# A scan layer followed by a gated feed-forward layer on one core: decay rows copied in the layout they are read in, and scan work moved between VectorE and GpSimd

## The chip, the cores and the metric

The kernel runs on one core of one Trainium2 chip. The core has TensorE (PE, with its weight loads shown apart as PEld), VectorE (DVE), ScalarE (ACT), GpSimd (POOL) and SyncE (SP, which here only issues transfers). The metric is the device time of one execution in microseconds, the median of several runs.

## What is computed

The first layer is a chunked scan of the Mamba-2 kind over 4 batches x 8 heads, sequences of 768 positions, head size 32 and state size 16. The second layer multiplies each of the 3072 rows of 256 by w_in, gates the result with its cosine, and multiplies it by w_out.

```python
batch, n_heads, seq, head_dim, d_state = (4, 8, 768, 32, 16)
for c in range(nc):
    cum = np.cumsum(la, axis=-1)                       # la = log(clip(a)) in the chunk
    M = einsum('bhin,bhjn->bhij', Cc, Bc) * exp(cum_i - cum_j) * causal
    y_intra = einsum('bhij,bhjd->bhid', M, xc)
    y_inter = einsum('bhin,bhnd->bhid', Cc, state) * exp(cum)[..., None]
    y[:, :, sl] = y_intra + y_inter
    Bx = einsum('bhjn,bhjd->bhjnd', Bc, xc) * exp(cum_last - cum_j)
    state = exp(sum(la)) * state + sum(Bx, axis=2)
x = y.transpose(0, 2, 1, 3).reshape(3072, 256)
h = x @ w_in                                           # 256 x 2048
out = (h * np.cos(h)) @ w_out                          # 2048 x 256
```

All of it is in 32-bit floating point.

## The kernel before

The sequence is cut into 6 chunks of 128 positions, each of two units of 64 (W). One chunk of the scan gives yT, the transposed input of the feed-forward layer for 4 x 128 rows. The feed-forward layer of chunk c runs in 16 steps, n = 16c + f with f from 0 to 15, and while it runs, the scan of chunk c+1 is threaded between its operations. One loop over n (L1114) records the instructions of all engines; each engine then works through its own list in that order, and waits only for data and for buffers.

One step n of the feed-forward layer:

- first(n) (L662): TensorE multiplies a block of w_in with one unit of yT into hp(n), one PSUM bank. Two banks take turns, so hp(n+2) needs hp(n) to have been read for the last time. In the runs of steps listed in `runs` (L1034) first7 (L757) does it instead, with 7 products of 128x128 in place of 8, a fast matrix multiplication. It reads differences of weights (wid, from differ_in, L734 on, made by GpSimd) and differences of y (yd, from differ_y, L745). A step belongs to unit f // 8 of the chunk, so the runs f = 9 to 13 of chunks 2 to 4 read the differences of the second unit only; the last run (steps 81 to 93) reads both.
- wind_k (ScalarE, L679), wind_w (VectorE, L685) and gate (ScalarE, L694) bring hp into range and take the cosine; gated (VectorE, L699) multiplies it with hp into gT(n). From chunk 1 on differ(n) (GpSimd, L724, L726, L727) forms the differences gd(n).
- second(n) runs two steps later. For chunk 0 it is a plain product with w_out (L808), after that seven (L848), whose products are read in the order 1, 2, 6, 7, 5, 4, 3 (1, 2, 7, 5, 6, 4, 3 in a run); products 1 and 2 need gT, 7, 5 and 6 need the first two operations of gd. After the last step of a unit ScalarE copies the sums out of PSUM into ps (L860, L861), and `rest` (L868) adds them up in four operations (L873), which the loop hands to GpSimd one per step where it can (L1197 on), or all four to VectorE.

The scan of a chunk from chunk 2 on:

- a is clipped into la and cut (L951 on), stored to memory (a_all, a_cut) and read back broadcast over partitions. load_arow reads the decays of one unit, from which decays0 scans lam (VectorE, L387). load_along reads whole chunks; `reaches` (L579) scans exp(cum) out of them, two scans of 64 per sequence (L586).
- turn_blocks transposes B and C (VectorE, L594), turn2 cuts C for the two heads of a strip (ScalarE, L603) and makes rT, the product of C with the reach (VectorE, L605). inner2 forms the inner products, weights (VectorE, L477) multiplies them with lam.
- add_state (VectorE, L510) adds the decayed state of the unit before, in four operations. open2 and finish2 sum y in PSUM, which ScalarE copies to yT.

Chunks 0 and 1 come from unit-wise functions. reach_unit (L439) scans the reach of one of the units 2 and 3 at a time, at step 9 and step 17, from alongs that load_unit_along filled.

`steps` (L1006) is a table written by hand: for each chunk the step f at which each piece is recorded. Work on VectorE in a step stands in the list `behind`: one piece before gated, the others after it.

Of the kernel before, what the change touches and what calls it, by code (L numbers as in the profile page):

```python
# [25 lines left out]
def kernel(  # L26
# [51 lines left out]
    ones = const.tile([P, P], FP32, name="ones")  # L78
    V.memset(ones, 1.0)
# [10 lines left out]
    a_all = dram.tile([NB, H, S], FP32, name="a_all")  # L90
    a_cut = dram.tile([NB, H, S], FP32, name="a_cut")
# [68 lines left out]
    def load_arow(k):  # L160

        arows[k] = t = rows.tile([P, H, P], FP32, tag="arow", name="arow").rearrange(
            "p h i -> p (h i)").rearrange("p (q h i) -> p q h i", q=2, h=H)
        i = k % 2
        if i:
            G.memset(t[:, :, :, 0:1], 0.0)
        for s in range(2):
            nc.sync.dma_start(
                out=t[s * W:(s + 1) * W, :, :, i:].rearrange("p q h i -> p (q h) i"),
                in_=a_cut[2 * s:2 * s + 2, :, k * W + i:(k + 1) * W].rearrange("q h i -> (q h) i")  # L170
                .unsqueeze(0).to_broadcast([W, 2 * H, W - i]))

    def load_unit_along(k):

        for p in range(2):
            for s in range(2):
                nc.sync.dma_start(
                    out=alongs[k][:, 2 * p + s, 1:],
                    in_=a_all[2 * s + p, :, k * W:(k + 1) * W].unsqueeze(1).to_broadcast([H, N, W]))

    def load_along(c, seqs=range(NB)):

        if c >= NC:
            return
        if c not in along:
            along[c] = rows.tile([P, NB, P], FP32, tag="along", bufs=2, name="along")
        for b in seqs:
            s = b // 2
            for qs, rs in turns_of[s]:
                hs = slice(2 * qs.start, 2 * qs.stop)  # L190
                nc.sync.dma_start(
                    out=along[c][rs, b], in_=a_all[b, hs, c * P:(c + 1) * P].unsqueeze(1)
                    .to_broadcast([hs.stop - hs.start, N, P]))
# [7 lines left out]
    lead, along1, reach1 = (ms[2][:, i * NB * (W + 1):(i + 1) * NB * (W + 1)]  # L201
                            .rearrange("p (b i) -> p b i", b=NB) for i in range(3))
    reachs = {1: reach1, 2: along1, 3: reach1}
    alongs = {k: ms[3][:, (k - 2) * NB * (W + 1):(k - 1) * NB * (W + 1)]
              .rearrange("p (b i) -> p b i", b=NB) for k in (2, 3)}
# [89 lines left out]
    for s in range(2):  # L295
        load_x(1, s)
    fetch("out", 0)
    nc.sync.dma_start(
        out=a_in, in_=a.rearrange("(u b) h (c p) -> (b h c) u p", u=NU, p=P))
# [80 lines left out]
    def decays0(k, p, i=0, n=1):  # L380

        if p == i == 0:
            lams[k] = scan.tile([P, 2, H, W], FP32, tag="lam", bufs=4, name="lam")
        flat = "p h i -> p (h i)"
        hs = slice(i * H // n, (i + 1) * H // n)
        rows_ = spread.pop((k, p, i)) if k < 2 else arows[k][:, p]
        V.tensor_tensor_scan(out=lams[k][:, p, hs].rearrange(flat), data0=rows_.rearrange(flat),  # L387
                             data1=unit0[:, hs].rearrange(flat), initial=0.0,
                             op0=ALU.mult, op1=ALU.add)
# [49 lines left out]
    def reach_unit(k):  # L439

        flat = "p b i -> p (b i)"
        V.tensor_tensor_scan(
            out=reachs[k].rearrange(flat), data0=alongs[k].rearrange(flat),
            data1=lead.rearrange(flat), initial=0.0, op0=ALU.mult, op1=ALU.add)

    def turn_unit(k):

        tp = pair("tp")[:, 0].rearrange("p (k q i) -> p k q i", k=2, q=2)
        for i, of in enumerate((bs, cs)):
            for p in range(2):  # L450
                PE.transpose(tp[:, i, p], of[k][:, p], ident)  # L451
        bTs[k] = scan.tile([P, 2, 2, P], FP32, tag="turned", bufs=2, name="turned0")[:, 0]
        ACT.copy(out=bTs[k], in_=tp[:, 0])
        cuts[k] = scan.tile([P, 2, 2, P], FP32, tag="cT2", bufs=2, name="cT2")
        for t in range(2):
            ACT.activation(cuts[k][:, t], tp[:, 1], AF.Copy, scale=slot[:, t:t + 1])
        rTs[k] = t = scan.tile([P, NB, W], FP32, tag="rT", name="rT")
        V.tensor_tensor(out=t, in0=tp[:, 1].rearrange("p q (s i) -> p (q s) i", s=2),
                        in1=reachs[k][:, :, 1:], op=ALU.mult)
# [45 lines left out]
    def add_state(k):  # L505

        for s in range(2):
            for p in range(2):
                i = k % 2 * W + W - 1
                V.scalar_tensor_tensor(out=after[k][:, s, p], in0=after[k - 1][:, s, p],  # L510
                                       scalar=reach[k // 2, s][:, p, i:i + 1],
                                       in1=after[k][:, s, p], op0=ALU.mult, op1=ALU.add)

    def finish0(k):
# [44 lines left out]
        def add():  # L559
            dec = scan.tile([P, 2, 2, 2 * D], FP32, tag="whole", bufs=1, name="whole")  # L560
            r4 = reachs[k].rearrange("p (q s) i -> p s q i", s=2)
            for s in range(2):
                G.tensor_tensor(out=dec[:, s], in0=old[:, s],
                                in1=r4[:, s, :, W:].to_broadcast([P, 2, 2 * D]), op=ALU.mult)
# [14 lines left out]
    def reaches(c, b):  # L579

        s, p = divmod(b, 2)
        if p == 0:
            reach[c, s] = scan.tile([P, 2, P], FP32, tag="reach", name="reach")
        for k in range(2):
            i = slice(k * W, (k + 1) * W)
            V.tensor_tensor_scan(out=reach[c, s][:, p, i], data0=along[c][:, b, i],  # L586
                                 data1=ones[:, 0:W], initial=1.0, op0=ALU.mult, op1=ALU.mult)

    turned, ys = {}, {}
# [8 lines left out]
    def turn2(c, s):  # L598

        tp = turned.pop((c, s))  # L600
# [3 lines left out]
        rT = scan.tile([P, 2, P], FP32, tag="rT", name="rT")  # L604
        V.tensor_tensor(out=rT, in0=tp[:, 1], in1=reach[c, s], op=ALU.mult)  # L605
        part[c, s] = (tp[:, 0], cT, rT)

    def inner2(c):

        g = [pair("g") for _ in range(2)]  # L610
        for k, p, s, q in ((k, p, s, q) for k in range(2) for p in range(2) for s in range(2)
                           for q in range(4)):
            bT, cT, _ = part[c, s]
# [9 lines left out]
    def open2(c):  # L623

        ys[c] = y = [pair("y") for _ in range(2)]
        for k, p, s, q in ((k, p, s, q) for k in range(2) for p in range(2) for s in range(2)
# [3 lines left out]
                      rhs=part[c, s][2][r, p, k * W:(k + 1) * W], start=(k == p == 0), stop=False,  # L630
# [4 lines left out]
    def finish2(c):  # L635

        y = ys.pop(c)
# [107 lines left out]
    def differ_y(c, i, eng, us=slice(0, 2)):  # L745
# [6 lines left out]
        a_ = (y12, y22, y22, y21)[i]  # L752
# [195 lines left out]
    la = const.tile([RB, NU, P], FP32, name="la")  # L948
    cut = const.tile([RB, NU, P], FP32, name="cut")

    def clip_cut():  # L951
        G.tensor_scalar(out=cut, in0=a_in, **clip)
        G.memset(cut[:, :, 0:1], 0.0)
        store_a(a_cut, cut)

    def clip_all():
        G.tensor_scalar(out=la, in0=a_in, **clip)

    def store_a(dst, src):
        nc.sync.dma_start(  # L960
            out=dst.rearrange("(u b) h (c p) -> (b h c) u p", u=NU, p=P), in_=src)
# [16 lines left out]
    def rest_of_loads():  # L978
        store_a(a_all, la)
# [7 lines left out]
        load_unit_along(2)  # L987
# [9 lines left out]
        load_unit_along(3)  # L997
        for s in range(2):
            load_x(3, s)
        for k in (4, 5):  # L1000
            for s in range(2):
# [4 lines left out]
    steps = {c: dict(reach=(5, 6), turn=(6, 7), inner=8, weigh=(9, 10), state=(-NF, 12),  # L1006
                     decays=(8, 11, 13, 14), along=(12, 13)) if c == 2 else
             dict(reach=(1, 2), turn=(3, 4), inner=5, weigh=(6, 7), state=(0, 5),
                  decays=(2, 8, 14, 15), along=(6, 7)) for c in range(2, NC)}
# [24 lines left out]
    runs = [*(range(NF * c + 9, NF * c + 14) for c in range(2, NC - 1)),  # L1034
            range(NC * NF - 15, NC * NF - 2)]
    sevens = {n: r for r in runs for n in r}
    late, at_ = [], {}

    def first_of_seven(n):
# [7 lines left out]
        to_ = at_["hp"] if i % 3 == (n > NF * (NC - 1)) else bank([P, TB], "hp", "h")  # L1047
# [63 lines left out]
    for k in (2, 3):  # L1111
        G.memset(alongs[k][:, :, 0:1], 0.0)
    rest_of_loads()
    for n in range(AHEAD, NC * NF + LAG):  # L1114
        c, f = divmod(n, NF)
        if n < NC * NF:
# [9 lines left out]
            if n in (NF - 1, NF):  # L1126
                load_along(2, (2 * (n == NF), 2 * (n == NF) + 1))
            for e, i in chunks_at(n, "along"):
                load_along(e + 1, (2 * i, 2 * i + 1))
# [9 lines left out]
            take_y = finish2(c + 1) if closing else None  # L1139
            if n not in sevens:  # L1140
# [4 lines left out]
            for e, s in chunks_at(n - 1, "turn"):  # L1145
                turn2(e, s)
            for k in units_at(n, 2):
# [10 lines left out]
            if joins:  # L1158
# [4 lines left out]
            behind += [lambda k=2 * c - 1 + i: add_state(k) for c, i in chunks_at(n, "state")]  # L1163
            behind += [lambda c=c, b=2 * s + p: reaches(c, b) for c, s in chunks_at(n, "reach")
                       for p in range(2)]
# [28 lines left out]
            for i, at in enumerate((4, 5, 6, 6) if 2 <= c < NC - 1 else ()):  # L1194
                if at == f:
                    differ_y(c, i, G, slice(1, 2))
            if unsummed and (c > 1 or summed[0]):  # L1197
# [13 lines left out]
        for start, js in zip((2 * NF - 5, 3 * NF - 3, 4 * NF - 3),  # L1211
                             (slice(1, 6), slice(0, 1), slice(6, NJ))):
# [21 lines left out]
        for k in units_at(n, 1):  # L1234
            reach_unit(k)
# [37 lines left out]
```

## Time and profile before

| | |
|---|---|
| three runs | 364.08, 364.23, 365.22 us |
| profiled execution | 364.44 us, its span 362.7 us, TensorE clock granted 0.998 |
| TensorE busy | 357.0 us (98%), 4070 matmul records |
| VectorE busy | 276.0 us (76%), 504 |
| ScalarE busy | 184.0 us (51%), 352 |
| GpSimd busy | 239.7 us (66%), 387 |
| transfers | 96624 packets, 26.43 MB, of which 86624 under 512 B |

Each 32-bit product counts as two records in the trace. The span is cut in stretches by chunk below: busy us of each engine.

| stretch, us | TensorE | VectorE | ScalarE | GpSimd |
|---|---|---|---|---|
| 0 to 17.7 | 16.05 | 14.00 | 7.60 | 9.70 |
| 17.7 to 81 | 63.14 | 52.96 | 42.64 | 46.30 |
| 81 to 140 | 59.00 | 47.39 | 27.33 | 44.52 |
| 140 to 197 | 57.00 | 42.48 | 27.64 | 38.19 |
| 197 to 254 | 57.00 | 42.51 | 27.60 | 38.10 |
| 254 to 311 | 57.00 | 40.26 | 26.19 | 33.34 |
| 311 to 362.7 | 47.84 | 36.42 | 24.99 | 29.54 |

In a timeline each line has the start, the duration, the engine, the line of the kernel, the operation, the tile written and those read, the shapes and the count of merged instructions; in brackets the idle time before it and what ended that.

### The profile page before, as it was taken

Reading aid. Unit: us, or ns where it says so; the run is one execution under the profiler, and the core shown is the slowest. Engines: PE = TensorE matmul, PEld = TensorE weight load, DVE = VectorE, ACT = ScalarE, POOL = GpSimd, SP = SyncE. Lnnn points to the kernel's source line nnn. Section 1 sums busy time; section 2 is a strip of 40 time slices with the busy share of each in tenths; the row PEclk is TensorE's granted clock in tenths of the full one; section 3 lists DMA queues with packets and bytes.
Section 4 is the critical chain, followed back from the end, with each engine's and each line's share of the span. In section 5 each row is a group of like instructions: output and inputs, shape, how many; then the busy total and the mean of one; then the engine's idle time right before and its main releaser. Section 6 shows DMA issues by size and latency. Waiting matters only on the chain.

```text
span 362.7 us, 10240 instructions
## 1 busy us (share of the span) xinstructions
PE 357.0 (98%) x4070; PEld 326.0 (90%) x4070; DVE 276.0 (76%) x504; ACT 184.0 (51%) x352; POOL 239.7 (66%) x387
## 2 busy tenths in 40 slices
PE   8999999999999999999999999999999999999995
PEld 4788888889999999999989999999999999999995
DVE  7779998488876987878766877875776776688864
ACT  3597656544454346534536533545553544444552
POOL 5567767699666677674786666686666465475572
PEclk9999999999999999999999999999999999999999
DMA  7984997666583429113228202110001001001001
GB/s 138 246 284 141 189 196 122 85 125 98 134 129 58 99 51 135 14 34 76 53 53 119 23 3 75 28 33 11 0 2 31 0 3 33 0 3 29 3 17 44
DMA packets 96624, 26.43 MB, mean 73 GB/s; under 512 B 86624, under 2 KB 92480, under 8 KB 96576
## 3 DMA queue, kind: packets, MB, share of 16 engines
q1 hardware_dynamic: 95328, 25.38, 34.9%
q8 instruction: 32, 0.52, 0.6%
q10 hardware_dynamic: 1248, 0.39, 0.5%
q14 instruction: 16, 0.13, 0.1%
HBM read 22.36 MB, written 3.34 MB: 71 GB/s over the span
## 4 chain that ended last, share of the span: by engine, by line
PE 96%; DMA 2%; DVE 1%; issue 0%; ACT 0%; POOL 0%; DVEq 0%
PE o L848 35%; PE hp L672 33%; PE o L808 8%; PE m L772 7%; PE hp L772 5%; DMA bc<-in_C_dram 2%; PE y L641 2%; PE g L615 1%; PE y L489 1%; PE y L629 1%; PE g L468 1%; PE y L537 1%; PE y L527 1%; PE o L900 0%; PE tp L451 0%
## 5 line engine op out<-in xcount | busy, mean ns | idle before, releaser
L672 PE MATMUL hp<-yT,w_in 128*128 128x256 f32 x544 | 129.6, 382 | 0.1
L672 PEld LDWEIGHTS hp<-yT,w_in 128*128 128x128 f32 x544 | 99.0, 190 | 13.8 <-issue 1.4
L724 POOL TENSOR_TENSOR gd<-gT 128x256 f32<-128x256 f32 x79 | 58.1, 735 | 76.9 <-DVE gT L699 61.8
L694 ACT ACTIVATE w<-w,quarter 128x512 f32<-128x512 f32 x96 | 69.4, 723 | 65.8 <-DVE w L685 65.7
L685 DVE SCALAR_TENSOR_TENSOR w<-hp,k 128x512 f32<-128x512 f32 x96 | 65.8, 686 | 45.4 <-ACT k L679 45.2
L679 ACT ACTIVATE k<-hp 128x512 int32<-128x512 f32 x96 | 57.2, 596 | 68.6 <-PE hp L672 60.3
L699 DVE TENSOR_TENSOR gT<-hp,w 128x512 f32<-128x512 f32 x96 | 65.6, 683 | 12.2 <-ACT w L694 8.3
L848 PE MATMUL o<-words,gd 128*128 128x128 f32 x474 | 66.0, 275 | 0.0
L848 PEld LDWEIGHTS o<-words,gd 128*128 128x128 f32 x474 | 59.4, 192 | 0.0
L848 PE MATMUL o<-w_out,gT 128*128 128x128 f32 x316 | 50.4, 278 | 0.0
L848 PEld LDWEIGHTS o<-w_out,gT 128*128 128x128 f32 x316 | 45.4, 191 | 3.1
L726 POOL TENSOR_TENSOR gd<-gT,gd 128x128 f32<-128x128 f32 x79 | 39.6, 501 | 6.2
L727 POOL TENSOR_TENSOR gd<-gT,gd 128x128 f32<-128x128 f32 x79 | 39.0, 493 | 6.2
L848 PE MATMUL o<-w_out,gd 128*128 128x128 f32 x158 | 30.6, 276 | 0.0
L848 PE MATMUL o<-words,gT 128*128 128x128 f32 x158 | 30.6, 275 | 0.0
L808 PE MATMUL o<-w_out,gT 128*128 128x256 f32 x128 | 30.0, 380 | 0.0
L387 DVE TENSOR_TENSOR_SCAN lam<-arow,unit 128x512 f32<-128x512 f32 x20 | 29.9, 1496 | 0.1
L808 PEld LDWEIGHTS o<-w_out,gT 128*128 128x128 f32 x128 | 24.2, 190 | 3.6 <-POOL w_out L283 0.4
L848 PEld LDWEIGHTS o<-words,gT 128*128 128x128 f32 x158 | 24.0, 192 | 0.0
L848 PEld LDWEIGHTS o<-w_out,gd 128*128 128x128 f32 x158 | 24.0, 192 | 0.0
L772 PE MATMUL m<-m,words 128*128 128x128 f32 x168 | 23.4, 276 | 0.0
L772 PE MATMUL hp<-yT,w_in 128*128 128x128 f32 x112 | 21.7, 275 | 0.0
(130 smaller groups left out, 463.6 us busy)
## 6 DMA issues: line engine op xcount, KB each, us to landing
words<-in_moe_w_in_dram SPq DMA_DIRECT2D x8, 512.0 KB
words<-in_moe_w_out_dram SPq DMA_DIRECT2D x8, 512.0 KB
xr<-in_x_dram SPq DMA_DIRECT2D x24, 128.0 KB
arow<-a_cut SPq DMA_DIRECT2D x10, 256.0 KB
arow<-a_cut SPq DMA_DIRECT2D x10, 252.0 KB
out_dram<-sum SPq DMA_DIRECT2D x18, 128.0 KB
bc<-in_B_dram SPq DMA_DIRECT2D x24, 64.0 KB
blocks<-in_B_dram SPq DMA_DIRECT2D x16, 32.0 KB
```

The source lines that it names most:

```text
L387: V.tensor_tensor_scan(out=lams[k][:, p, hs].rearrange(flat), data0=rows_.rearrange(flat), data1=unit0[:, hs].rearrange(flat), initial=0.0 ...
L672: PE.matmul(to_[:, e], lhsT=w_in[:, k, fs], rhs=y[:, k], start=(k == 0), stop=(k == KT - 1), skip_group_check=True)
L679: ACT.activation(k, hp[n], AF.Copy, bias=0.25, scale=INV_2PI)
L685: V.scalar_tensor_tensor(out=w, in0=hp[n], scalar=INV_2PI, in1=k, op0=ALU.mult, op1=ALU.subtract)
L694: ACT.activation(cos, cos, AF.Sin, bias=quarter, scale=TWO_PI)
L699: V.tensor_tensor(out=gT[n], in0=hp.pop(n), in1=cos, op=ALU.mult)
L724: G.tensor_tensor(out=d[:, 0:2], in0=g[:, 1:2].to_broadcast([P, 2, P]), in1=g[:, 3::-3], op=ALU.subtract)
L726: G.tensor_tensor(out=d[:, 2], in0=g[:, 0], in1=d[:, 0], op=ALU.subtract)
L727: G.tensor_tensor(out=d[:, 3], in0=g[:, 2], in1=d[:, 2], op=ALU.subtract)
L772: PE.matmul(dst[q], lhsT=w[q], rhs=y_[q], start=(q in (6, 1, 7)), stop=True, skip_group_check=True)
L808: PE.matmul(o[c, u][:, t], lhsT=g[:, 2 * e + t], rhs=w_out[:, 2 * j + e], start=(j == e == t == 0), stop=(j == NJ - 1 and e == 1), skip_gr ...
L848: PE.matmul(at[q], lhsT=a_[q], rhs=w[q], start=(j == 0 and q in starts), stop=(j == NJ - 1), skip_group_check=True)
```

## The change

- *Copies of a.* a_all and a_cut get new layouts in memory. A row of a_all holds, for a chunk and a pair of sequences, four units of 64 with one element ahead of each (set to 0 in la), so 260 elements in a row; a row of a_cut holds the decays of all 8 heads of a unit. They are read back in rows of 1040 and 2048 bytes. The memsets of arow and of alongs go; a_in is loaded by four transfers, la is stored by two.
- *Reach.* The scan runs over 260 elements at once, restarted by the tile lead (1 ahead of each unit, 0 elsewhere), for a pair of sequences. A chunk needs two such scans instead of eight of 64. For units 2 and 3 reach_unit(s) does pair s for both units, at steps 9 and 10.
- *State and rT on GpSimd.* From chunk 3 on add_state2 multiplies the old state by its decay and, a step later, adds it: two GpSimd operations of 128x256 for four on VectorE. rT becomes scale2, on GpSimd from chunk 3 on.
- *Differences of y.* In chunks 2 to 4 those of the second unit stay on GpSimd, at f = 1 and 2 instead of 4 to 6. Those of the first unit are added, on VectorE at f = 0, from PSUM.
- *Sums.* The condition under which `rest` goes to GpSimd leaves out f = 2, 3, 4 after chunk 1; where it does not hold, the branch below it gives all four operations to VectorE (outside a run of seven).
- *Order.* From chunk 3 on: reach at f = 5, 6 (1, 2 before), transposes at -1, 1 (3, 4), cuts at 3, 4 (4, 5), rT at 6, 7 (4, 5), state at 2, 7 (0, 5), the first scan of lam at 5 (2). The differences of weights for columns 1 to 5 are made in three pieces instead of one.

```diff
     def load_arow(k):
-        arows[k] = t = rows.tile([P, H, P], FP32, tag="arow", name="arow")...
-        i = k % 2
-        if i:
-            G.memset(t[:, :, :, 0:1], 0.0)
-        for s in range(2):
+        arows[k] = t = rows.tile([P, 2, H * W], FP32, tag="arow", name="arow")
+        for q in range(2):
             nc.sync.dma_start(
...
+                out=t[:, q],
+                in_=a_cut[:, k % 2, q, k // 2].unsqueeze(1).to_broadcast([2, W, H * W]))
...
+    def add_state2(k):
+        dec = scan.tile([P, 2, 2, 2 * D], FP32, tag="whole", bufs=1, name="whole")
+        flat = "p s q d -> p (s q) d"
+        G.tensor_tensor(out=dec.rearrange(flat), in0=after[k - 1].rearrange(flat),
+                        in1=reach[k // 2][:, :, k % 2, W:].to_broadcast([P, NB, 2 * D]),
+                        op=ALU.mult)
+        return lambda: G.tensor_tensor(out=after[k], in0=after[k], in1=dec, op=ALU.add)
...
+    def reaches(c, s):
+        if s == 0:
+            reach[c] = scan.tile([P, NB, 2, W + 1], FP32, tag="reach", bufs=1, name="reach")
+        V.tensor_tensor_scan(
+            out=reach[c][:, 2 * s:2 * s + 2].rearrange("p b k i -> p (b k i)"),
+            data0=along[c][:, s],
+            data1=lead.rearrange("p b i -> p (b i)"), initial=0.0, op0=ALU.mult, op1=ALU.add)
...
+    def scale2(c, s, eng):
+        r2[c, s] = rT = scan.tile([P, 2, P], FP32, tag="rT", name="rT")
+        eng.tensor_tensor(out=rT.rearrange("p q (k i) -> p q k i", k=2),
+                          in0=turned.pop((c, s))[:, 1].rearrange("p q (k i) -> p q k i", k=2),
+                          in1=reach[c][:, 2 * s:2 * s + 2, :, 1:], op=ALU.mult)
...
-             dict(reach=(1, 2), turn=(3, 4), inner=5, weigh=(6, 7), state=(0, 5),
-                  decays=(2, 8, 14, 15), along=(6, 7)) for c in range(2, NC)}
+             dict(reach=(5, 6), turn=(-1, 1), cut=(3, 4), scale=(6, 7), inner=5, weigh=(6, 7),
+                  state=(2, 7), decays=(5, 8, 14, 15), along=(6, 7)) for c in range(2, NC)}
...
+            for i in range(4 if f == 0 and 2 <= c < NC - 1 else 0):
+                differ_y(c, i, V, slice(0, 1), ypsum)
...
-            for i, at in enumerate((4, 5, 6, 6) if 2 <= c < NC - 1 else ()):
+            for i, at in enumerate((1, 1, 2, 2) if 2 <= c < NC - 1 else ()):
                 if at == f:
                     differ_y(c, i, G, slice(1, 2))
-            if unsummed and (c > 1 or summed[0]):
+            for e, s in chunks_at(n, "scale"):
+                if e > 2:
+                    scale2(e, s, G)
+            for add in adds:
+                add()
+            adds[:] = [add_state2(2 * e - 1 + i) for e, i in chunks_at(n, "state") if e > 2]
+            if unsummed and (c > 1 and f not in (2, 3, 4) or summed[0]):
                 unsummed[0](range(summed[0], summed[0] + 1), G)
...
-        for start, js in zip((2 * NF - 5, 3 * NF - 3, 4 * NF - 3),
-                             (slice(1, 6), slice(0, 1), slice(6, NJ))):
+        for start, js in zip((2 * NF - 5, 2 * NF - 1, 2 * NF + 8, 3 * NF - 3, 4 * NF - 3),
+                             (slice(2, 5), slice(1, 2), slice(5, 6), slice(0, 1), slice(6, NJ))):
```

## The prediction

> **What bounds the kernel now.** I read the busy shares and the slices first, then the chain of waits, then the list of waits, and last the timelines of single engines around the places that the diff edits.
>
> ```profile
> PE 357.0 (98%) x4070; PEld 326.0 (90%) x4070; DVE 276.0 (76%) x504; ACT 184.0 (51%) x352; POOL 239.7 (66%) x387
> PE   8999999999999999999999999999999999999995
> PE 96%; DMA 2%; DVE 1%; issue 0%; ACT 0%; POOL 0%; DVEq 0%
> ```
>
> TensorE is busy in all but the first and the last slice, and the chain that ended last is TensorE for 96%. Cut into stretches, the windows show TensorE busy for 16.05 of the first 17.7 us, for 63.14 of the next 63.3, for every one of the 57.00 us of each later chunk, and for 47.84 of the last 51.7. Its clock is granted at 0.998. So from 17.7 us on there is next to nothing to win: the waits of TensorE behind another engine after that point are these.
>
> ```profile
> PEld o L808 <- POOL w_out L283: 0.4, 1, 0.4
> ...
> PEld y L527 <- DVE w L685: 0.3, 1, 0.3
> ...
> PEld hp L672 <- DVE gT L699: 0.3, 1, 0.3
> ```
>
> With two of 0.2 us on the first products of hp they make 1.4 us, all in chunk 0. The diff adds, drops and reorders no TensorE instruction. What it can do is make TensorE wait. So the question at each edit is a margin: how long before TensorE reads a tile does VectorE or GpSimd finish it?
>
> Two margins recur in each step of 3.29 us. VectorE multiplies gT(n) out of the PSUM bank that TensorE needs for hp(n+2), and GpSimd forms gd(n) from gT(n) (L724, L726, L727) for the products o(n), two steps later. The chunk taken for the working is chunk 3; chunks 2 and 4 run the same 57 us earlier and later.
>
> ```profile
> 197.34 0.69 DVE L685 SCALAR_TENSOR_TENSOR w<-hp,k 128x512 f32<-128x512 f32 x1 [1.05 <-ACT k L679]
> ...
> 198.89 0.69 DVE L699 TENSOR_TENSOR gT<-hp,w 128x512 f32<-128x512 f32 x1
> ...
> 205.93 0.68 DVE L699 TENSOR_TENSOR gT<-hp,w 128x512 f32<-128x512 f32 x1
> ```
>
> Step 49 (first three fields: start, duration, engine) shows that from the start of w to the end of gT takes 199.58 - 197.34 = 2.24 us, sine on ScalarE included. gT(51) ends at 206.61, and hp(53) starts at 207.88 in TensorE's timeline: a margin of 1.2 us.
>
> **The change part by part.** The sum is made against the profiled execution, 364.44 us (span 362.7 and 1.7 around it); the median of the runs shown is 0.2 us lower.
>
> *Start.* VectorE loses the memset of ones (0.17 us). It sits ahead of a copy (L324, 1.83 to 2.42) that runs until GpSimd's own copy is done (2.34), and the chain goes through the transfer of C until 6.9 us. So 0 to -0.17; I take 0. The load of a_in becomes four: three more at 0.47 us (its row on SP) push the following fetches by 1.4 us. The first of these, issued at 13.17, is read by ScalarE at 22.55, after other work without a wait; on SP nothing else is queued behind but fetches read later still. 0; bare of that cover, at most 1.4 once.
>
> *Chunk 0.* The one scan that served unit 3 at step 17 (L442) moves to step 10, as two scans of a pair each now serve units 2 and 3. It stands between gT(10) and w(11). The row is 1.15 us in the mean, from 0.67 (L429, fed from PSUM) to 1.39. Before rT of step 11 VectorE idles 0.3 us for ScalarE, and gT(11), at 59.27, is 1.2 us ahead of hp(13). Even 1.39 - 0.3 = 1.1 fits. 0. GpSimd loses memsets of arow (0.12 each) and gains one strided memset of la (0.35, by that of cut), ahead of the w_out piece on which TensorE waits 0.4: -0.1 to +0.2, I take 0.
>
> *Transfers.* arow comes in rows of 2 KB where it came in rows of 256 B, along in 1040 B where it was 512 B. After 6.9 us TensorE waits for no transfer, so 0. The blocks of sequences must land earlier: turn_blocks moves to f = -1 and 1, its last load is issued at 189.5 and read at about 198. Small-packet traffic ahead of it shrinks; 0.
>
> *Step 48 (f = 0).* Between gT(47) and w(48) come two transposes (1.13 the pair) and four differences read from PSUM; the nearest row is L785, 128x128 with one operand in PSUM, 0.29. 1.13 + 4 x 0.29 = 2.3 us against 2.06 us of idle time there. w(48) is 0.2 us later, with 1.6 us of margin, and the state additions (0.95 here) behind it are gone. In chunk 2 the idle time is 1.3, so w(32) is 1.0 later, of which 0.6 is won back since the four state additions between w and gT (1.55) go. 0. Those four results have no reader in chunks 2 to 4: the runs of seven products cover steps f = 9 to 13 only, which read the second half.
>
> *Step 50 (f = 2).* Here the new condition on f sends the four sums of the last output (L873) past GpSimd to VectorE, between gT(50) and w(51); a wait of w(51) holds ScalarE's sine, gT(51) and hp(53). The scan of lam goes from this step, so gT(50) ends at 200.60 (k ready) + 2.27 (step 49: 197.31 to 199.58) = 202.87. The nearest row for the sums is four VectorE operations of 128x256, all in SBUF, right behind a gT and with a gd beside them:
>
> ```profile
> 304.17 0.69 DVE L699 TENSOR_TENSOR gT<-hp,w 128x512 f32<-128x512 f32 x1 [1.33 <-ACT w L694]
> 304.78 1.28 DVE L754 TENSOR_TENSOR m<-yT 128x256 f32<-128x256 f32 x2
> 305.98 1.27 DVE L754 TENSOR_TENSOR m<-yT,m 128x256 f32<-128x256 f32 x2
> 307.17 0.68 DVE L685 SCALAR_TENSOR_TENSOR w<-hp,k 128x512 f32<-128x512 f32 x1
> ```
>
> That is 2.39 us. w(51) starts at 202.79 + 2.39 = 205.18, gT(51) ends at 207.42, hp(53) at 207.88 does not wait: 0, with 0.4 to spare. The low bound is four at 0.42 (rT, L605, alone): also 0. The high bound is the row of the same sums in chunk 1:
>
> ```profile
> 126.97 0.56 DVE L873 TENSOR_TENSOR sum<-ps 128x256 f32<-128x256 f32 x1
> 127.57 2.98 DVE L873 TENSOR_TENSOR sum<-ps,sum 128x256 f32<-128x256 f32 x3
> ```
>
> 3.5 us there, beside a GpSimd difference of 1.73 us. By it gT(51) ends at 208.53, 0.7 us late, three times: +2.1. I take 0, since beside these sums run only gd and short differences, as at 304.
>
> [...]
>
> *Steps 53 to 56 (f = 5 to 8).* The reach scan of the second pair stands before w(55), where VectorE idles 0.45: 1.15 - 0.45 = 0.7 us later, gT(55) 221.3 instead of 220.66. GpSimd's queue up to gd(56) then is
>
> ```profile
> 220.80 0.73 POOL L724 TENSOR_TENSOR gd<-gT 128x256 f32<-128x256 f32 x1 [0.55 <-DVE gT L699]
> 221.61 0.46 POOL L726 TENSOR_TENSOR gd<-gT,gd 128x128 f32<-128x128 f32 x1
> 222.14 0.46 POOL L727 TENSOR_TENSOR gd<-gT,gd 128x128 f32<-128x128 f32 x1
> 223.76 0.64 POOL L393 TENSOR_TENSOR sc<-bc,lam 128x256 f32<-128x256 f32 x1 [1.16 <-DVE lam L387]
> 225.78 0.73 POOL L724 TENSOR_TENSOR gd<-gT 128x256 f32<-128x256 f32 x1 [1.39 <-PE o L848]
> ```
>
> with rT, the decayed state and its addition added, each 0.73 (L566, 128x256). gd(55) from 221.4 for 1.8 us; the scan lam(56) now falls on it and holds one of its operations by 0.8 (an L726 at 125.47 took 1.25 beside a scan, 0.46 alone); then 3 x 0.73 + 0.64: 226.8, where gd(56) started at 225.78. TensorE reads its first part at 227.66: 226.8 + 0.73 = 227.5, just in time. Chunk 2 has one more difference of weights there (128x128, 0.46): 0.4 late. Chunk 4 has no sc: early. Sum +0.4. Bounds: without the collision 0; with two collisions 1.2 + 0.8 + 0.2 = 2.2.
>
> In all 364.44 + 0.4 = 364.84 by the profiled execution, 364.6 by the median.
>
> **The rivals.** (1) No change that can be told from none, as worked out. For it: 1.2 to 1.6 us of margin nearly everywhere, and a TensorE that did not wait before.
> (2) Slower through VectorE: the sums at f = 2 become the bound from 2.8 us on, when w(51) starts after 205.6. At the row of chunk 1, 364.2 + 2.1 + 0.4 = 366.7. For it: the only row of these very instructions. Against: the 1.73 us GpSimd difference beside it there.
> (3) Slower through GpSimd: gd(40), gd(56) and gd(72) late by two collisions each, 364.2 + 2.2 = 366.4. For it: the queue is full to 0.1 us. [...]
> (4) Faster: lighter transfers and GpSimd memsets take away the waits of chunk 0 and nothing else is lost: 364.2 - 1.4 = 362.8 for all of them, 363.5 for half. Against: the scan added at step 10 and the unchanged order of the w_out additions.
>
> **How the numbers follow.** What a measurement of this kernel tells from no change is about 0.3%, 1.1 us: below 363.1 is faster, above 365.3 slower. Chances: (1) 0.54, (2) 0.20, (3) 0.16, (4) 0.10. Of (4) 0.07 lies below 363.1; the rest joins (1) as no change, 0.57, and (2) and (3) make 0.36 for slower. The price is that of (1), 364.6. The range reaches down to half of (4), 363.5, and up to (2), 366.7.
>
> **What would show it.** After: TensorE's instruction count and busy time the same within 0.5 us; no wait of hp on gT at steps 37, 53, 69; sums of about 2.4 us on VectorE at f = 2; gd(40) starting at about 170.4 with o(40) waiting some 0.4 for it. The forecast is wrong if TensorE shows gaps over 0.5 us at f = 4 or 8, or if the time to 17.7 us moves by more than 0.3.

## The result, and the profile after

The changed kernel takes 403.19 us (median of four runs, 399.88 to 404.71), where the kernel before took 364.55 beside it: a ratio of 1.105 (95% interval 1.098 to 1.112), slower by about 39 us. The profiled execution is 403.34 us with a span of 401.5. The forecast was 364.6, and all of its four cases lie below 367.

The page of the changed kernel: its busy times, three rows of its 40 slices (PE, TensorE's busy share in tenths; PEclk, the clock it was granted, in tenths of full speed; DMA, the mean busy share of the 16 DMA engines) and the chain that ended last:

```profile
PE 369.8 (92%) x4070; PEld 334.6 (83%) x4070; DVE 267.5 (67%) x473; ACT 183.5 (46%) x352; POOL 243.4 (61%) x395
...
PE   8999879895579988969999989999999999999996
...
PEclk9999999997869998978999999999999999999999
DMA  7883493711261261224511244200101001000102
...
PE 60%; DMA 13%; SPq 13%; DVE 4%; issue 3%; POOL 3%; ACT 3%; DVEq 0%; ACTq 0%; POOLq 0%
```

The chain was TensorE for 96% and is so for 60%; transfers (DMA) and SP's issuing of transfers (SPq) have taken 13% each. The number of matmul records is the same. The holes in TensorE's row lie in slices 5 to 24 of 10 us each, that is between 40 and 241 us, and through most of them the DMA engines are busy for one to four tenths. So transfers are late while most DMA engines are idle. What the engines wait for, in the list of waits (total, times, longest):

```profile
DVE lam L376 <- DMA arow<-a_cut: 19.2, 5, 7.9
...
PE hp L672 <- DVE gT L699: 16.3, 8, 4.7
...
DVE turned L589 <- DMA blocks<-in_C_dram: 6.8, 2, 3.5
PE g L478 <- DMA xr<-in_x_dram: 6.7, 2, 6.5
...
ACT mag L245 <- DMA words<-in_moe_w_out_dram: 6.5, 2, 6.0
...
ACT mag L245 <- DMA words<-in_moe_w_in_dram: 6.2, 2, 3.3
```

None of these transfers appears in the waits of the kernel before. arow is one that the diff edits; blocks, xr and words are not, nor were their bytes changed. SyncE's timeline around the first two loads of arow:

```profile
33.91 1.17 SPq L163 DMA_DIRECT2D arow<-a_cut  x2
35.20 2.84 SPq L221 DMA_DIRECT2D words<-in_moe_w_in_dram  x1
38.09 7.22 SPq L107 DMA_DIRECT2D bc<-in_B_dram  x2
```

The two loads are issued in 1.17 us (1.30 in the kernel before). The two issues of bc behind them take 7.22, against 2.35 in the kernel before: SP is held up. What the DMA engines do meanwhile is seen in the view of the transfers, cut to 36 to 38 us (packets; then queue, packets, MB, share of 16 engines):

```profile
DMA packets 50, 0.10 MB, mean 51 GB/s; under 512 B 0, under 2 KB 0, under 8 KB 50
...
q1 hardware_dynamic: 50, 0.10, 13.1%
```

13.1% of 16 engines is 2.1 engines. Those were busy for 0.131 x 16 x 2 us = 4.2 us with 50 packets of 2 KB: 0.084 us each. The two loads of a unit are 256 such packets, by estimate 256 x 0.084 / 2 = 10.7 us on two engines. In the diff, the source of one load was [64 copies, 16 rows, 64] and is now [2, 64 copies, 512]: its slowest dimension counts 2, as many as the engines that are busy. That gave the author's theory for the experiments, not shown up to here: the loads of arow run on 2 of the 16 engines because of that 2, and other transfers that need these two, and SP's queue behind them, come late. Loads that keep only so few engines busy are called confined below.

A transfer that the diff leaves alone is late in landing as well, not in its issue only:

```profile
49.22 0.66 ACT L245 ACTIVATE mag<-words 128x512 f32<-128x512 f32 x1 [3.28 <-DMA words<-in_moe_w_in_dram]
```

This is the twelfth piece of weights that ScalarE reads, and the twelfth that is fetched is the one whose issue ended at 38.04 above. It landed some 11.2 us after that; in the kernel before the same piece is read at 44.89 without a wait.

The path from a late load to the end, in the timelines of VectorE and TensorE:

```profile
93.71 1.22 DVE L376 TENSOR_TENSOR_SCAN lam<-arow,unit 128x512 f32<-128x512 f32 x1 [7.87 <-DMA arow<-a_cut]
94.85 0.67 DVE L699 TENSOR_TENSOR gT<-hp,w 128x512 f32<-128x512 f32 x1
```

```profile
85.99 1.89 PE L672 MATMUL hp<-yT,w_in 128*128 128x256 f32 x8
...
95.57 3.78 PE L672 MATMUL hp<-yT,w_in 128*128 128x256 f32 x8 [4.73 <-DVE gT L699]
```

The scan of lam stands ahead of gT on VectorE and waits 7.87 us; hp waits for gT 4.73 us. Then the eight matmul records of a step's hp take 3.78 us, twice the 1.89 that they took at 85.99. TensorE's granted clock, the third number from the end in these windows of the changed kernel, was 1.00 in the pause and is 0.50 after it:

```profile
92.00:94.00 2.00, 0.00 (x0) 0.00 (x0) 0.29 (x1) 0.00 (x0) 0.00 (x0) 1.00 0.15 46
...
96.00:98.00 2.00, 2.00 (x6) 1.55 (x6) 0.45 (x2) 0.72 (x1) 1.23 (x3) 0.50 0.16 58
...
102.00:104.00 2.00, 2.00 (x13) 1.82 (x12) 0.00 (x0) 0.35 (x2) 1.15 (x3) 1.00 0.15 55
```

The windows of 81 to 140 us in the kernel before, and then in the changed one (PE busy and records first, then the other engines, granted clock, DMA share, GB/s):

```profile
81.00:140.00 59.00, 59.00 (x854) 54.10 (x854) 47.39 (x73) 27.33 (x57) 44.52 (x66) 1.00 0.57 100
```

```profile
81.00:140.00 59.00, 46.83 (x487) 41.48 (x487) 29.39 (x44) 20.92 (x41) 31.47 (x50) 0.86 0.26 66
```

So the 38.8 us of span split in two: TensorE idles 31.7 us of 401.5 instead of 5.7 of 362.7 (26.0 more), and it is busy 369.8 instead of 357.0 with the same products (12.8 more), which fits the granted clock of 0.86 here and 0.966 over the span (369.8 x 0.966 = 357.2).

### The profile page after: what moved, and what is told of

The parts are those of the page before. It is cut to its first block, busy times and chain, and to the rows that moved or that the text cites. A ratio compares the mean times of both kernels' runs of the same rounds, so it can differ in the third digit from the quotient of the medians.

```text
span 401.5 us, 10176 instructions
## 1 busy us (share of the span) xinstructions
PE 369.8 (92%) x4070; PEld 334.6 (83%) x4070; DVE 267.5 (67%) x473; ACT 183.5 (46%) x352; POOL 243.4 (61%) x395
## 2 busy tenths in 40 slices
DMA packets 76735, 26.48 MB, mean 66 GB/s; under 512 B 65136, under 2 KB 70032, under 8 KB 76688
## 4 chain that ended last, share of the span: by engine, by line
PE 60%; DMA 13%; SPq 13%; DVE 4%; issue 3%; POOL 3%; ACT 3%; DVEq 0%; ACTq 0%; POOLq 0%
PE o L849 26%; PE hp L672 19%; PE m L773 6%; SPq L150 5%; PE hp L773 4%; DMA arow<-a_cut 4%; SPq L107 4%; DMA blocks<-in_C_dram 4%; DMA words<-in_moe_w_out_dram 2%; DMA xr<-in_x_dram 1%; DMA words<-in_moe_w_in_dram 1%; PE g L615 1%; DVE w L685 1%; DVE gT L699 1%; SPq L177 1%
## 5 line engine op out<-in xcount | busy, mean ns | idle before, releaser
L672 PE MATMUL hp<-yT,w_in 128*128 128x256 f32 x544 | 136.5, 397 | 16.3 <-DVE gT L699 16.3
L672 PEld LDWEIGHTS hp<-yT,w_in 128*128 128x128 f32 x544 | 102.7, 198 | 33.2 <-DVE gT L699 11.1
L849 PE MATMUL o<-words,gd 128*128 128x128 f32 x474 | 67.8, 280 | 0.9 <-POOL gd L726 0.7
L849 PEld LDWEIGHTS o<-words,gd 128*128 128x128 f32 x474 | 61.0, 196 | 1.5 <-POOL gd L726 1.2
L849 PE MATMUL o<-w_out,gT 128*128 128x128 f32 x316 | 51.7, 284 | 0.0
L849 PEld LDWEIGHTS o<-w_out,gT 128*128 128x128 f32 x316 | 46.8, 197 | 3.5
L727 POOL TENSOR_TENSOR gd<-gT,gd 128x128 f32<-128x128 f32 x79 | 39.2, 497 | 6.2
L376 DVE TENSOR_TENSOR_SCAN lam<-arow,unit 128x512 f32<-128x512 f32 x20 | 27.7, 1385 | 19.2 <-DMA arow<-a_cut 19.2
L809 PEld LDWEIGHTS o<-w_out,gT 128*128 128x128 f32 x128 | 24.2, 190 | 3.7 <-POOL w_out L270 0.5
```

What stands on the lines that cost most here:

```text
L672: PE.matmul(to_[:, e], lhsT=w_in[:, k, fs], rhs=y[:, k], start=(k == 0), stop=(k == KT - 1), skip_group_check=True)
L727: G.tensor_tensor(out=d[:, 3], in0=g[:, 2], in1=d[:, 2], op=ALU.subtract)
L809: PE.matmul(o[c, u][:, t], lhsT=g[:, 2 * e + t], rhs=w_out[:, 2 * j + e], start=(j == e == t == 0), stop=(j == NJ - 1 and e == 1), skip_gr ...
L849: PE.matmul(at[q], lhsT=a_[q], rhs=w[q], start=(j == 0 and q in starts), stop=(j == NJ - 1), skip_group_check=True)
```

## The experiments

**1. The changed kernel with arow cut by halves of the partitions.** Bytes, 2 KB rows and the number of transfers stay; only the order in which the two loads divide the work changes.

```diff
-        for q in range(2):
+        for s in range(2):
             nc.sync.dma_start(
-                out=t[:, q],
-                in_=a_cut[:, k % 2, q, k // 2].unsqueeze(1).to_broadcast([2, W, H * W]))
+                out=t[s * W:(s + 1) * W],
+                in_=a_cut[s, k % 2, :, k // 2].unsqueeze(0).to_broadcast([W, 2, H * W]))
```

> The changed kernel with one edit: the two loads of arow per unit are cut by halves of the partitions instead of by q, so that the source's slowest dimension counts 64 and not 2. Rows stay 2 KB, bytes and number of transfers stay. Theory (the loads of arow run on 2 of 16 DMA engines, and all transfers that share these two, and the SP queue behind, come late): the 2 KB packets spread over the engines, no wait of the scan of lam on arow over 1 us, and the time is 363.5 to 366, the rest of the change being worth what the prediction's sum said, +0.4. Rival A (the longer rows of arow, or the layout of a in DRAM, delay the transfers whatever their engines): 395 to 405, nothing changes. Rival B (the moves between VectorE and GpSimd cost most of the 39 us): 385 to 405.

Measured: 364.48 us, 1.0016 of the kernel before (1.0007 to 1.0025; 363.95 beside it). Of the 39 us 38.7 are gone. The windows of 36 to 38 us in this kernel, and then in the changed one (the last two columns are DMA share and GB/s):

```profile
36.00:38.00 2.00, 2.00 (x10) 1.54 (x9) 2.00 (x4) 1.73 (x4) 1.31 (x2) 1.00 0.95 205
```

```profile
36.00:38.00 2.00, 2.00 (x10) 1.52 (x9) 2.00 (x3) 1.79 (x4) 1.31 (x2) 1.00 0.13 51
```

15.2 engines (0.95 x 16) are busy in place of 2.1. SP is not held either: in this kernel's SP timeline the same two issues of bc take 1.32 us, not 7.22.

```profile
33.84 1.34 SPq L163 DMA_DIRECT2D arow<-a_cut  x2
35.30 0.52 SPq L221 DMA_DIRECT2D words<-in_moe_w_in_dram  x1
35.86 1.32 SPq L107 DMA_DIRECT2D bc<-in_B_dram  x2
```

**2. The kernel before with this one load alone.** It takes over a_cut's layout, the order of a_in that goes with it (four loads of a_in, four stores of a_all) and load_arow, and drops the memsets of arow. The copy that along reads, and all moves between engines, are left out.

```diff
-    a_cut = dram.tile([NB, H, S], FP32, name="a_cut")
+    a_cut = dram.tile([2, 2, 2, NC, H * W], FP32, name="a_cut")
...
-        for s in range(2):
+        for q in range(2):
             nc.sync.dma_start(
-                out=t[s * W:(s + 1) * W, :, :, i:].rearrange("p q h i -> p (q h) i"),
...
+                out=t[:, q],
+                in_=a_cut[:, k % 2, q, k // 2].unsqueeze(1).to_broadcast([2, W, H * W]))
```

> The kernel before with the changed kernel's a_cut, a_in and load of arow alone (2 KB rows, source [2, 64 copies, 512]); the copy of a that along reads keeps its layout and its 512 B rows, and all the moves of VectorE and GpSimd are left out. Theory: this edit alone costs nearly the whole difference, 390 to 405 us, with waits of several us of lam on arow and of xr, blocks and words on their transfers. Rival B (moves between engines): 363.5 to 367. Rival C (two causes that add: the loads of arow and the earlier reading of blocks by turn_blocks): 375 to 390 here.

Measured: 401.46 us, ratio 1.103 (1.100 to 1.105). From its list of waits:

```profile
DVE lam L384 <- DMA arow<-a_cut: 22.3, 5, 8.9
```

One edit alone costs what the whole change costs. With experiment 1 it is shown from both sides that this load is the cause. Neither the longer rows nor the work moved between VectorE and GpSimd is, since experiment 1 keeps both.

**3. Which property of the load counts.** Three variants of experiment 1, in which each half of 64 partitions is cut once more; the diff is that of 62 and 2.

```diff
         for s in range(2):
-            nc.sync.dma_start(
-                out=t[s * W:(s + 1) * W],
-                in_=a_cut[s, k % 2, :, k // 2].unsqueeze(0).to_broadcast([W, 2, H * W]))
+            for lo, hi in ((0, 62), (62, W)):
+                nc.sync.dma_start(
+                    out=t[s * W + lo:s * W + hi],
+                    in_=a_cut[s, k % 2, :, k // 2].unsqueeze(0).to_broadcast([hi - lo, 2, H * W]))
```

> The kernel of the first run (loads of arow cut by halves of the partitions, 16 engines), with each half cut once more, into 62 and 2 partitions. The two transfers more per unit cost 2 x 0.5 us of issue on SP. [...] Rival A (what counted in the changed kernel was that the slowest dimension was short, 2, or that copies stood behind it): a slowest dimension of 62 spreads, 364 to 367.

> [...] Rival A: 364 to 367.

> [...] Rival A: 364 to 367.

| partitions of the loads | engines busy from 36 to 38 us (DMA share x 16) | us | ratio (95%) |
|---|---|---|---|
| 128 in two rows of 64 copies (the change) | 2.1 | 403.19 | 1.105 (1.098 to 1.112) |
| 62 and 2 | 2.1 | 406.74 | 1.117 (1.111 to 1.124) |
| 57 and 7 | 6.6 | 375.24 | 1.031 (1.028 to 1.034) |
| 49 and 15 | 9.0 | 364.41 | 1.001 (1.000 to 1.002) |
| 64 (experiment 1) | 15.2 | 364.48 | 1.0016 (1.0007 to 1.0025) |

The windows of 36 to 38 us of the kernels with 62 and 2, with 57 and 7, and with 49 and 15:

```profile
36.00:38.00 2.00, 2.00 (x9) 1.54 (x10) 1.97 (x4) 1.97 (x4) 1.31 (x2) 1.00 0.13 46
```

```profile
36.00:38.00 2.00, 2.00 (x10) 1.53 (x9) 2.00 (x4) 1.74 (x4) 1.31 (x2) 1.00 0.41 108
```

```profile
36.00:38.00 2.00, 1.91 (x9) 1.44 (x8) 1.97 (x4) 2.00 (x5) 1.31 (x3) 1.00 0.56 177
```

With a slowest dimension of 62 again only 0.13 x 16 = 2.1 engines are busy, although it is long. The two transfers more per unit are not the reason: 49 and 15 has them too. So length alone does not tell, and no run here shows what sets 62 apart from 64. In the windows of the last three kernels of the table other transfers may run beside the loads, and the traces do not show which engines a load runs on. The loss goes with these shares, but not in proportion to them: against experiment 1 it is 42 us at 2.1 engines, 11 us at 6.6, and nothing at 9.0.

**4. The loads of arow issued from ScalarE.** The same loads as in the change, but not in SP's queue.

```diff
-            nc.sync.dma_start(
+            nc.scalar.dma_start(
                 out=t[:, q],
```

> The changed kernel as it is (2 engines), with the loads of arow issued from ScalarE instead of SP. Theory that what hurts is the sharing of the two engines (every other transfer has its part on them): the others land as late as before, 385 to 405. Rival (what hurts is SP's queue, which stands still while the loads are outstanding): SP runs on, 365 to 378. ScalarE pays 0.55 us for each issue, 1.1 us per unit, and waits where a tile of arow isn't free; that can add some us to both.

Measured: 403.29 us (1.108, 1.105 to 1.111), no gain. From ScalarE's timeline, and then SP's:

```profile
31.91 11.34 ACTq L163 DMA_DIRECT2D arow<-a_cut  x4
```

```profile
71.50 6.50 SPq L107 DMA_DIRECT2D bc<-in_B_dram  x4
78.04 7.94 SPq L150 DMA_DIRECT2D blocks<-in_B_dram  x2
```

Now ScalarE is held at its own issues, and SP still is, behind loads that are not in its queue (two issues of blocks take 7.94 us at 78.04 and 1.12 us at 86.03). That is in keeping with shared engines, which no trace shows directly. But ScalarE lost time of its own, so the 403.29 us can't be put down to them alone. The next run leaves out another cause, the wait for the confined load itself.

**5. A copy that nobody reads.** The kernel reads arow as in experiment 1, and issues each load once more into a piece of DRAM that nothing reads: once in the form of the change, once, as the control, by halves of the partitions.

```diff
+        for q in range(2):
+            spare = dram.tile([2, W, H * W], FP32, name=f"spare{k}{q}")
+            nc.sync.dma_start(
+                out=spare, in_=a_cut[:, k % 2, q, k // 2].unsqueeze(1).to_broadcast([2, W, H * W]))
```

> The first run's kernel (arow read on 16 engines) with every load of arow issued once more behind it, into a piece of DRAM that nothing reads, in the changed kernel's form (source [2, 64 copies, 512], two transfers per unit). So nothing waits for what runs on the two engines. Theory (other transfers that have a part on these engines, and SP's queue behind them, come late): 380 to 405, with waits on words, xr, blocks and arow. Rival (the loss was the wait of the scan of lam for its own slow load): 364 to 367. If both count: 367 to 380.

> The control of the run before: the same unread second copy of every load of arow, the same bytes and 2 KB packets, but cut by halves of the partitions, so that it runs on 16 engines. Theory (it is the confinement to two engines): 364 to 368. Rival (it is the traffic of 0.5 MB more per unit, or the two issues more): 390 to 415.

Measured: 414.72 us (1.139, 1.130 to 1.148) in the form of the change, more than expected; 364.80 us (1.0016, 1.0005 to 1.0027) by halves. The first of them waits for transfers none of which is the confined one:

```profile
PE g L482 <- DMA xr<-in_x_dram: 16.1, 2, 15.9
DVE lam L380 <- DMA arow<-a_cut: 10.0, 2, 8.3
ACT mag L249 <- DMA words<-in_moe_w_out_dram: 9.3, 3, 7.8
```

Same bytes, same packets, no reader, and the two forms lie 50 us apart. So here the confined load harms the transfers beside it, even where its own lateness harms nobody. These copies stand in SP's queue, so the run doesn't divide the harm between transfers that land late and an SP that issues late. Both occur (the landing 11.2 us after the issue, the issues of 7.22 us), and no run separates their shares. Why it is 414.7 and not 405 stays open.

**6. Confined loads late in the kernel only.** Units 8 to 11 (4 of 10 loaded units) in the form of the change, the others as in experiment 1.

```diff
+        if k >= 8:
+            for q in range(2):
+                nc.sync.dma_start(
+                    out=t[:, q],
+                    in_=a_cut[:, k % 2, q, k // 2].unsqueeze(1).to_broadcast([2, W, H * W]))
+            return
```

> The first run's kernel with the changed kernel's load of arow (2 engines) for units 8 to 11 alone, 4 of the 10 loaded units, whose loads are issued from about 130 us on, where the DMA engines are busy for 0.33 of the time and less. If each confined load costs the same: 364.5 + 0.4 x 39 = 380. Theory (a confined load costs where other transfers with near due times are queued on the same two engines): 364.5 to 367.

Measured: 368.15 us (1.011, 1.004 to 1.018), 3.7 above experiment 1: less than a share of 0.4, but more than the theory said. One wait makes it, in the timelines of VectorE and TensorE:

```profile
202.49 0.63 DVE L595 STREAM_TRANSPOSE turned<-blocks 128x256 f32<-128x256 f32 x1 [3.72 <-DMA blocks<-in_C_dram]
```

```profile
203.70 3.68 PE L678 MATMUL hp<-yT,w_in 128*128 128x256 f32 x8 [2.05 <-DVE gT L705]
```

TensorE waits 2.05 us for it, and the eight records of hp then take 3.68 in place of 1.89: together 3.8 us. This transpose stands where the diff moved turn_blocks (f = 1). In SP's timeline its last load comes right behind two confined ones:

```profile
188.48 1.11 SPq L164 DMA_DIRECT2D arow<-a_cut  x2
189.64 2.64 SPq L153 DMA_DIRECT2D blocks<-in_C_dram  x1
```

So the earlier reading of blocks cost nothing that shows with the loads of experiment 1, and made this wait of 3.72 us with four units confined.

**7. The rest of the change.** Experiment 1 with the sums of f = 2 to 4 back on GpSimd and without the differences of the first half of y, which nothing reads.

```diff
-            for i in range(4 if f == 0 and 2 <= c < NC - 1 else 0):
+            for i in range(0):
...
-            if unsummed and (c > 1 and f not in (2, 3, 4) or summed[0]):
+            if unsummed and (c > 1 or summed[0]):
```

> As the first of these kernels, but with the sums of the last output at f = 2 to 4 back on GpSimd and without the differences of the first half of y, which nothing reads. Theory (these sit in idle time of VectorE, as the prediction's steps 48 and 50 say): within 0.3% of the first kernel. Rival (the prediction's second rival, VectorE at f = 2 is the bound): 2 us less than the first kernel.

Measured: 364.43 us (1.0015, 1.0006 to 1.0023), the same as experiment 1.

**8. A use for those differences.** Experiment 1 with runs of seven products at f = 2 to 4 as well; and the same with the sums on GpSimd from f = 3 on.

```diff
-    runs = [*(range(NF * c + f, NF * c + l) for c in range(2, NC - 1) for f, l in ((9, 14),)),
+    runs = [*(range(NF * c + f, NF * c + l) for c in range(2, NC - 1) for f, l in ((2, 5), (9, 14))),
...
# second kernel only
-            if unsummed and (c > 1 and f not in (2, 3, 4) or summed[0]):
+            if unsummed and (c > 1 and f != 2 or summed[0]):
```

> As the first of these kernels, with the runs of seven products at steps f = 2 to 4 of chunks 2 to 4 as well, for which the first halves of the differences of y are formed. Theory: nine steps lose one TensorE product group of about 0.165 us each, so TensorE is busy about 1.5 us less and the time is 362 to 364. Rival (the operations that the sevens add on VectorE and GpSimd at f = 2 to 4 are late for hp): 366 to 370.

> The third run's kernel (runs of seven products at f = 2 to 4 too), with the sums of the last output on GpSimd from f = 3 on instead of f = 5. There they ended at 227.47 in step f = 8 of chunk 3, ScalarE's copy of the next output waited 0.72 for them, and TensorE's o 0.88 for that copy; the same in chunk 2. Theory (those waits ate the nine shorter steps): 2 x 1.1 us back, 363.0 to 364.0. Rival (GpSimd's queue at f = 3 and 4 is full, gd late for o there): 365 to 367.

Measured: 365.54 us (1.0042, 1.0028 to 1.0056) for the first, a miss. Its timelines of GpSimd, ScalarE and TensorE, one line each:

```profile
227.02 0.45 POOL L874 TENSOR_TENSOR sum<-ps,sum 128x128 f32<-128x128 f32 x1
```

```profile
227.51 0.48 ACT L861 COPY ps<-o 128x384 f32<-128x384 f32 x1 [0.72 <-POOL sum L874]
```

```profile
228.04 0.71 PE L849 MATMUL o<-w_out,gT 128*128 128x128 f32 x4 [0.71 <-ACT ps L861]
```

With f = 2 to 4 in a run, neither engine took the sums there; GpSimd began them at f = 5, and the last one ended after the next output was ready for the same buffer. In the second kernel that last sum ends at 219.80, and the time is 362.86 us: 0.9974 of the kernel before (0.9962 to 0.9986; 363.97 beside it), the fastest kernel here.

## Why the prediction was wrong, step by step

**Transfers: the step that failed.** It said "arow comes in rows of 2 KB where it came in rows of 256 B", and from "After 6.9 us TensorE waits for no transfer" concluded 0. Bytes and row length were read out of the diff, the order of the dimensions was not. The slowest dimension of the loads went from 64 to 2, they ran on 2.1 engines, and the step is worth +38.7 us (experiment 1) instead of 0. Its remark that the small-packet traffic ahead of the blocks shrinks was true of the packets (96624 to 76735 in all) and pointed the wrong way: the fewer packets, on 2.1 engines, were more in the way than the many had been. A margin "no engine waits for a transfer" also had no size. It should have been asked what time each transfer takes, from issue to landing, and how many engines it keeps busy; the prediction asked neither.

**Start: small, but not settled.** The products of hp that begin at 17.67 us in the kernel before begin at 17.13 in the changed one. That is 0.54 earlier, beyond the 0.3 that the prediction gave as a sign of being wrong. But kernels with the same start as the changed one have them anywhere from 16.80 (experiment 7) to 17.57 (49 and 15), so single profiles can't place it.

**Chunk 0 and step 48: right.** From 17.7 to 81 us TensorE is busy 63.13 in experiment 1 (63.14 before), for all of the 59.00 us to 140, in which step 32 lies, and for 56.86 of the 57.00 to 197, in which step 48 lies; the 0.14 missing there belong to o(40) below.

**Step 50: right in size.** The sums on VectorE, in experiment 1:

```profile
202.57 0.42 DVE L874 TENSOR_TENSOR sum<-ps 128x256 f32<-128x256 f32 x1
203.03 1.89 DVE L874 TENSOR_TENSOR sum<-ps,sum 128x256 f32<-128x256 f32 x3
204.84 0.68 DVE L685 SCALAR_TENSOR_TENSOR w<-hp,k 128x512 f32<-128x512 f32 x1
```

From 202.57 to 204.92 is 2.35 us, by the row taken 2.39; hp(53) doesn't wait, and experiment 7 shows that taking the sums away wins nothing. In the profile of the changed kernel the sums of chunk 4 take 2.34 us (298.23 to 300.57), with GpSimd's three gd operations beside them from 298.46 to 300.43 (0.77, 0.52 and 0.52).

**Steps 53 to 56: right in size, in part by luck.** In experiment 1 TensorE's weight loads show the one wait that was named, o(40) in chunk 2:

```profile
170.52 0.74 PEld L849 LDWEIGHTS o<-words,gd 128*128 128x128 f32 x6 [0.33 <-POOL gd L726]
```

0.33 us, predicted 0.4. But gd itself starts at 169.20 and not at 170.4, and what TensorE waits for is its second operation, not the first as the prediction had it; the two errors nearly cancel. The collision with the scan of lam is there: in the profile of the changed kernel the L727 at 201.32 takes 1.36 us beside the scan at 201.23, where the middle one of 79 takes 0.46. The kernel of experiment 1 as a whole is +0.16%, about 0.6 us (0.3 to 0.9), which is near the +0.4 of the sum but isn't this step: 0.2 us of it lie outside the profiled span (2.0 us around the span on the mean, 1.8 in the kernel before beside it), where the prediction has no term.

**The rivals.** Of the two on the slow side, VectorE's sums fell with experiment 7, and GpSimd's queue cost 0.33 once and not 2.2. Neither concerned transfers. The prediction named transfers only among the gains, so no case led above 367. Of its own signs, TensorE's busy time told the failure apart: it moved by 12.8 us, not 0.5. Its gaps, up to 6.48 us, are far beyond 0.5 too; but behind most of them stand transfers (arow, blocks, xr, words, state), not the work of VectorE and GpSimd for which the sign was set at f = 4 and 8.

## What to carry to other kernels

Where a diff changes the layout of a transfer, write down source and destination as lists of counts, slowest first, before and after, and ask how many engines it will keep busy: here a slowest count of 2 took 39 us more than one of 64, with the same bytes, and 2.1 engines were busy in place of 15.2. Don't judge a transfer by its own reader alone: here a confined one delayed those beside it (a copy read by nobody cost 50 us). And do look at DMA share and issue times together: here it was told by 2.1 busy engines of 16 while two issues of the queue took 7.22 us. Work whose results have no reader may belong to a step that isn't switched on; with it on, and one buffer freed in time, the kernel was 0.26% faster than before.

## What the hardware showed that was not expected

- Cutting the same 64 copies into 62 and 2 made the kernel 42 us slower, and into 49 and 15 not at all. From 36 to 38 us 2.1 engines were busy with 62 and 15.2 with 64, so length alone does not tell.
- An issue had no fixed cost here: with confined transfers outstanding, two issues on SP took 7.22 us instead of 1.32, and four on ScalarE took 11.34 us.
- Late transfers were paid for twice here: after a pause of 4.73 us eight matmul records of hp took 3.78 us instead of 1.89, at a granted clock of 0.50 (in chunk 0, with pauses of up to 1.97 us, it stayed at 1.00), and a third of the whole loss (12.8 of 38.8 us of span) is TensorE at a lower granted clock.
